# Sine and product of a chunk issued two chunks behind its scaling instead of one

## The chip, the cores and the metric

One NeuronCore of one Trainium2 chip. The metric is the device time of one execution in microseconds; lower is better.

## The reference

A long convolution along the sequence, then a gated feed-forward layer on its output. Shapes: 4 sequences of 12480 positions, 128 channels; the layer has 2048 hidden units; all float32 (the layer's weights arrive as float64).

```python
h_filt = (np.maximum(pos_emb @ w1, 0.0) @ w2) * np.exp(-0.01 * pos)[:, None]
u = x * v
y = irfft(rfft(u, n=2*S) * rfft(h_filt, n=2*S))[:, :S, :]   # causal convolution
x2 = (x * y).reshape(49920, 128)
h = x2 @ w_in            # 128 -> 2048
g = h * np.cos(h)
out = g @ w_out          # 2048 -> 128
```

## The kernel before

The convolution of sequence 0 is done first, alone. From 635 us on, the layer runs over 104 tiles of 480 tokens, each in 16 **chunks** of 128 hidden units, and between its instructions the convolutions of sequences 1 to 3 are issued in small units. Each of those has five stages: U (load x and v, multiply, fold), F1 (first transform), F2 (second transform and product with the filter), I1 and I2 (back). After them comes a stretch with the layer alone, called plain below.

cos(h) is sin(2 pi f), with f the signed distance of h/(2 pi) + 1/4 from its nearest whole number. A chunk therefore goes through all the engines: matmul `ph` on TensorE (PE), scaling `a` on ScalarE (ACT), rounding `k` on VectorE (DVE), fraction `f` on GpSimd (POOL), sine `cs` on ACT, product `gt` on DVE, second matmul into `acc` on PE.

```python
ps_acc = tile_pool(name="ps_acc", bufs=2, space=PSUM)
ps_h = tile_pool(name="ps_h", bufs=4, space=PSUM)      # ph, and the transposes below
ps_c = tile_pool(name="ps_c", bufs=2, space=PSUM)      # the convolution's banks
# ... cut ...
def moe_turn(pool, n):                                 # input of tile n, transposed
    zb = zbs.pop(n)
    pt = ps_h.tile([P, BANK], F32, name="ph")          # borrows a ph
    # ... four transposes into pt, then DVE: at <- pt

def moe_up(pool, n, c):
    ph = ps_h.tile([P, BANK], F32, name="ph")
    nc.tensor.matmul(ph[:, 0:TOK], w_in_sb[:, c * P:(c + 1) * P], ats[n][:, :], ...)
    a = pool.tile([P, TOK], F32, name="a", bufs=3)
    nc.scalar.activation(a[:, :], ph[:, 0:TOK], AF.Identity, bias=quarter[:, 0:1], scale=INV_TWO_PI)
    k = pool.tile([P, TOK], F32, name="k")
    nc.vector.tensor_scalar(out=k[:, :], in0=a[:, :], scalar1=ROUND, scalar2=ROUND,
                            op0=ALU.add, op1=ALU.subtract)
    f = pool.tile([P, TOK], F32, name="f")
    nc.gpsimd.tensor_tensor(f[:, :], a[:, :], k[:, :], op=ALU.subtract)
    return ph, f

def moe_act(pool, ph, f):
    cs = pool.tile([P, TOK], F32, name="cs")
    nc.scalar.activation(cs[:, :], f[:, :], AF.Sin, scale=TWO_PI)
    gt = pool.tile([P, TOK], F32, name="gt", bufs=4)
    nc.vector.tensor_tensor(gt[:, :], ph[:, 0:TOK], cs[:, :], op=ALU.mult)   # last reader of ph
    return gt

# ... cut: moe_store borrows a ph too, for the transposes of a tile's output ...
for i in range(len(steps) + LAG):                      # LAG = 4
    if i < len(steps):
        n, c = steps[i]
        # ... load of tile n + 2 at c == 0 ...
        hidden[i] = moe_up(mpool, n, c)
    if 0 <= i - 1 < len(steps):
        gates[i - 1] = moe_act(mpool, *hidden.pop(i - 1))
    if i >= LAG:
        pn, pc = steps[i - LAG]
        moe_down(pn, pc, gates.pop(i - LAG))
        # ... copy of a finished tile to ot, on ACT ...
    if i < len(steps):
        if c == LAG + 1 and n - 1 in ots:
            moe_store(mpool, n - 1, ots.pop(n - 1))    # at position 5
        if c == NFC // 2 and n + 1 < NALL:
            moe_turn(mpool, n + 1)                     # at position 8
    owed += share
    while owed > 0.0:
        owed -= next(conv, owed)                       # units of the convolution
```

In U, a unit is one multiplication `xt` on DVE, then one sum on POOL and one difference on DVE into `slots`.

## Time and profile before

| | before |
|---|---|
| median time | 4257.37 us (3 runs, 4257.25 to 4261.64) |
| profiled span, granted TensorE clock | 4262.5 us, 0.954 |
| the layer with convolutions between, 635 to 3376 us | 1139 chunks |
| the layer alone, 3376 to 4251 us | 525 chunks, 1.67 us each |

Three ways of reading are used throughout. A row of the busy table by stretch has, after the stretch and its length, the busy time and number of instructions of PE, its weight loads, DVE, ACT and POOL, then the granted clock, the busy share of the DMA engines and their GB/s. A row of the waits says who stood still, what ended it, the total in us, how often, and the longest. A row of the timeline has start, duration, engine, line, operation, what it writes and reads, and in brackets how long its engine had been idle and what ended that. The lines that carry the argument are shown inside the prediction.

### The profile page before, as it was taken

How to read it: one execution, taken by the hardware profiler on the slowest of the kernel's cores; microseconds unless marked ns; L12 is line 12 of the kernel's file. 1: busy time of each engine (PE TensorE's matmuls, PEld its weight loads, DVE VectorE, ACT ScalarE, POOL GpSimd, SP SyncE). 2: the span in 40 equal slices, each digit the busy share in tenths (PEclk: the TensorE clock that was granted, in tenths of full speed). 3: DMA queues.
4: the chain of work that ended last, by engine and by line, in shares of the span. 5: the costliest groups of instructions: out<-in, count | busy, mean ns of one | idle time of the engine just before them, and what ended most of it. 6: DMA issues, size and time to landing. Idle time of an engine off the chain costs nothing.

```text
span 4262.5 us, 49170 instructions
## 1 busy us (share of the span) xinstructions
PE 3916.4 (92%) x13882; PEld 2244.3 (53%) x13882; DVE 3047.8 (72%) x6588; ACT 2415.2 (57%) x4484; POOL 2546.8 (60%) x2311
## 2 busy tenths in 40 slices
PE   5868778999999998998899989988999999999999
PEld 3836673554456653554466634644466644444444
DVE  8657669987778568777776588766675566666666
ACT  1343155775567445655455456644554577777777
POOL 2422347657865457568854476568754577777776
PEclk8557889999999999999999999999999999999999
DMA  3354343112211442012201531022103400000000
GB/s 86 89 167 120 96 136 106 50 52 78 82 51 42 142 142 85 15 50 81 75 12 51 177 112 42 15 73 78 52 15 107 127 19 19 19 19 19 19 19 14
DMA packets 271763, 293.63 MB, mean 69 GB/s; under 512 B 16741, under 2 KB 204101, under 8 KB 271237
## 3 DMA queue, kind: packets, MB, share of 16 engines
q1 hardware_dynamic: 271493, 290.50, 23.6%
q8 instruction: 112, 1.84, 0.2%
q14 instruction: 158, 1.29, 0.1%
HBM read 210.12 MB, written 80.31 MB: 68 GB/s over the span
## 4 chain that ended last, share of the span: by engine, by line
PE 65%; POOL 11%; DVE 10%; ACT 5%; DMA 5%; issue 3%; SPq 0%; DVEq 0%; POOLq 0%; ACTq 0%
PE ph L569 24%; PE acc L591 23%; POOL f L578 6%; POOL slots L369 5%; PE cv L404 4%; PE cv L386 4%; ACT cs L583 3%; PE cv L343 3%; PE ps L343 3%; DVE gt L585 2%; DMA w<-wd 2%; DMA hd<-h 2%; PE ph L116 2%; DVE slots L336 1%; PE ps L386 1%
## 5 line engine op out<-in xcount | busy, mean ns | idle before, releaser
L578 POOL TENSOR_TENSOR f<-a,k 128x480 f32<-128x480 f32 x1664 | 2021.9, 1218 | 1174.9 <-DVE k L575 1174.9
L569 PE MATMUL ph<-at,w_in_sb 128*128 128x480 f32 x3328 | 1647.4, 577 | 102.6 <-DVE gt L585 101.6
L591 PE MATMUL acc<-gt,w_out_sb 128*128 128x480 f32 x3328 | 1618.0, 568 | 0.5 <-DVE gt L585 0.5
L572 ACT ACTIVATE a<-ph,quarter 128x480 f32<-128x480 f32 x1664 | 1094.2, 658 | 750.7 <-PE ph L569 691.8
L585 DVE TENSOR_TENSOR gt<-ph,cs 128x480 f32<-128x480 f32 x1664 | 1091.7, 656 | 476.3 <-ACT cs L583 452.7
L583 ACT ACTIVATE cs<-f 128x480 f32<-128x480 f32 x1664 | 998.4, 600 | 690.6 <-POOL f L578 688.7
L575 DVE TENSOR_SCALAR k<-a 128x480 f32<-128x480 f32 x1664 | 778.8, 468 | 528.3 <-ACT a L572 514.4
L591 PEld LDWEIGHTS acc<-gt,w_out_sb 128*128 128x128 f32 x3328 | 633.8, 190 | 715.5 <-issue 713.5
L569 PEld LDWEIGHTS ph<-at,w_in_sb 128*128 128x128 f32 x3328 | 584.8, 191 | 575.4 <-issue 290.4
L369 POOL TENSOR_TENSOR slots<-slots,t 120x256 f32<-120x256 f32 x384 | 296.6, 795 | 228.2 <-DVE t L368 176.6
L357 PE MATMUL ps<-slots,w 124*120 124x256 f32 x384 | 165.9, 576 | 80.7 <-DVE w L250 45.6
L386 PEld LDWEIGHTS cv<-cs,slots 120*96 120x96 f32 x1536 | 180.5, 168 | 82.0 <-issue 72.1
L357 PE MATMUL cv<-slots,w 124*120 124x256 f32 x576 | 155.3, 390 | 49.7 <-PE acc L591 36.0
L404 PEld LDWEIGHTS cv<-slots,tm 96*104 96x104 f32 x1440 | 173.1, 171 | 46.7 <-issue 36.0
L386 PE MATMUL cv<-cs,slots 120*96 120x120 f32 x1536 | 191.2, 267 | 3.3 <-POOL slots L369 3.3
L404 PE MATMUL cv<-slots,tm 96*104 96x128 f32 x1440 | 178.7, 275 | 11.0 <-DMA tm<-td 7.2
L343 PEld LDWEIGHTS cv<-c,slots 104*124 104x124 f32 x768 | 130.6, 192 | 84.4 <-issue 54.8
L357 PEld LDWEIGHTS ps<-slots,w 124*120 124x120 f32 x384 | 93.0, 268 | 153.0 <-issue 70.5
L357 PEld LDWEIGHTS cv<-slots,w 124*120 124x120 f32 x576 | 98.7, 182 | 134.3 <-PE acc L591 78.0
L343 PE MATMUL cv<-c,slots 104*124 104x192 f32 x768 | 159.5, 330 | 3.2 <-POOL slots L336 2.6
L396 DVE TENSOR_TENSOR slots<-cv,other 96x240 f32<-96x240 f32 x384 | 135.9, 393 | 0.5
L330 POOL TENSOR_TENSOR xt<-xt,vt 104x512 f32<-104x512 f32 x30 | 38.3, 1276 | 137.5 <-DMA vt<-in_v_dram 127.0
(111 smaller groups left out, 2781.8 us busy)
## 6 DMA issues: line engine op xcount, KB each, us to landing
h<-hd SPq DMA_DIRECT2D x192, 240.0 KB
tm<-td SPq DMA_DIRECT2D x90, 312.0 KB
xt<-in_x_dram SPq DMA_DIRECT2D x120, 208.0 KB
vt<-in_v_dram SPq DMA_DIRECT2D x120, 208.0 KB
xs<-in_x_dram SPq DMA_DIRECT2D x120, 208.0 KB
zd<-zs SPq DMA_DIRECT2D x120, 208.0 KB
zb<-zd SPq DMA_DIRECT2D x104, 240.0 KB
out_dram<-ob SPq DMA_DIRECT2D x104, 240.0 KB
```

What stands on the lines that cost most here:

```text
L343: nc.tensor.matmul(ps[0:KE, i * 2 * N1:(i + 1) * 2 * N1], u[:, b, 0:KE, i], c1[0:u.shape[0], :, :].rearrange("p r k -> p (r k)"), start=Tr ...
L357: nc.tensor.matmul(ps[0:N2, i * 2 * D:(i + 1) * 2 * D], w[:, i, :], parts[0:KE, :, k1 + i, :, :], start=True, stop=True)
L369: nc.gpsimd.tensor_tensor(y[:, r], y[:, r], t[:, r], op=op)
L386: nc.tensor.matmul(ps[0:N1, (i * 2 + r) * N2:(i * 2 + r + 1) * N2], parts[0:N2, r, :, b, i], cs[:, r:r + 2, :].rearrange("p c a -> p (c a) ...
L404: nc.tensor.matmul(ps[0:R, i * D:(i + 1) * D], t[:, i, r, :], slots[0:N1, :, place, :], start=(r == 0), stop=(r == 1))
L569: nc.tensor.matmul(ph[:, 0:TOK], w_in_sb[:, c * P:(c + 1) * P], ats[n][:, :], start=True, stop=True)
L572: nc.scalar.activation(a[:, :], ph[:, 0:TOK], AF.Identity, bias=quarter[:, 0:1], scale=INV_TWO_PI)
L575: nc.vector.tensor_scalar(out=k[:, :], in0=a[:, :], scalar1=ROUND, scalar2=ROUND, op0=ALU.add, op1=ALU.subtract)
L578: nc.gpsimd.tensor_tensor(f[:, :], a[:, :], k[:, :], op=ALU.subtract)
L583: nc.scalar.activation(cs[:, :], f[:, :], AF.Sin, scale=TWO_PI)
L585: nc.vector.tensor_tensor(gt[:, :], ph[:, 0:TOK], cs[:, :], op=ALU.mult)
L591: nc.tensor.matmul(accs[n][:, 0:TOK], w_out_sb[:, c, :], gt[:, :], start=(c == 0), stop=(c == NFC - 1))
```

## The change

The sine and the product of chunk i-1 stood behind the scaling of chunk i. The intent is to give POOL one chunk more before ACT needs its f, so that ACT and DVE do not stand at the head of their queues waiting for it. The fraction and its rounding get a third buffer, since they now live longer.

```diff
     LAG = 4
+    SINE_LAG = 2
@@
-        k = pool.tile([P, TOK], F32, name="k")
+        k = pool.tile([P, TOK], F32, name="k", bufs=3)
@@
-        f = pool.tile([P, TOK], F32, name="f")
+        f = pool.tile([P, TOK], F32, name="f", bufs=3)
@@
-            if 0 <= i - 1 < len(steps):
-                gates[i - 1] = moe_act(mpool, *hidden.pop(i - 1))
+            if 0 <= i - SINE_LAG < len(steps):
+                gates[i - SINE_LAG] = moe_act(mpool, *hidden.pop(i - SINE_LAG))
```

All lines of the changed kernel from here on are one further down: line 572 before is 573 after.

## The prediction

> **What bounds the kernel now.** I read the page's busy shares first, then the busy time by stage, then the waits of the stages where TensorE has gaps, then the timeline of one period in each.
>
> ```profile
> PE 3916.4 (92%) x13882; PEld 2244.3 (53%) x13882; DVE 3047.8 (72%) x6588; ACT 2415.2 (57%) x4484; POOL 2546.8 (60%) x2311
> ```
>
> TensorE (PE) leads, but 92% is a mean over stages. The gated layer (1664 chunks of 480 tokens, 16 chunks to a tile, 104 tiles) runs from 635 us to the end. Until about 3376 us the three remaining convolutions are interleaved with it, each in five stages. Busy time of the second convolution's stages, one row each: loading and folding (U), first transform (F1), second transform with product (F2), back transforms (I1, I2), and last the stretch with no convolution left ("plain"). Columns: stretch, length, then busy us of PE, PE's weight loads, DVE, ACT, POOL.
>
> ```profile
> 1543.00:1695.00 152.00, 126.34 (x304) 51.72 (x302) 132.70 (x202) 80.47 (x139) 111.54 (x97) 0.99 0.35 102
> 1696.00:1865.00 169.00, 168.71 (x593) 100.57 (x592) 125.69 (x284) 113.04 (x219) 91.11 (x77) 1.00 0.06 15
> 1869.00:2125.00 256.00, 232.40 (x676) 118.49 (x676) 181.31 (x411) 128.07 (x222) 206.10 (x200) 1.00 0.28 78
> 2135.00:2313.00 178.00, 177.69 (x845) 111.33 (x844) 125.72 (x285) 105.64 (x219) 92.11 (x78) 1.00 0.04 12
> 2320.00:2453.00 133.00, 132.49 (x683) 91.66 (x684) 69.32 (x126) 56.15 (x95) 55.15 (x46) 0.97 0.58 172
> 3400.00:4200.00 800.00, 800.00 (x2165) 387.78 (x2164) 555.27 (x1022) 611.29 (x993) 579.62 (x481) 1.00 0.07 19
> ```
>
> F1, I1, I2 and the plain stretch are full of matmuls; only U (126 of 152) and F2 (232 of 256) have gaps. The activation of line 572 runs once a chunk: 68, 75, 107, 75, 46 and 481 times in these stretches, so a chunk takes 2.24, 2.25, 2.39, 2.37, 2.89 and 1.66 us. The waits of F2 say why it is slow:
>
> ```profile
> ACT cs L583 <- POOL f L578: 112.8, 62, 2.8
> DVE gt L585 <- ACT cs L583: 69.1, 47, 1.7
> ```
>
> and its timeline shows a closed loop:
>
> ```profile
> 2002.07 1.58 POOL L369 TENSOR_TENSOR slots<-slots,t 120x256 f32<-120x256 f32 x2 [0.97 <-PE acc L591]
> ...
> 2003.61 2.55 POOL L578 TENSOR_TENSOR f<-a,k 128x480 f32<-128x480 f32 x2
> ...
> 2005.03 0.60 ACT L583 ACTIVATE cs<-f 128x480 f32<-128x480 f32 x1 [2.75 <-POOL f L578]
> ...
> 2005.66 0.66 DVE L585 TENSOR_TENSOR gt<-ph,cs 128x480 f32<-128x480 f32 x1 [1.72 <-ACT cs L583]
> ...
> 2006.24 0.41 DVE L367 TENSOR_TENSOR slots<-cv,h 120x256 f32<-120x256 f32 x1
> ...
> 2007.13 1.59 POOL L369 TENSOR_TENSOR slots<-slots,t 120x256 f32<-120x256 f32 x2 [0.97 <-PE acc L591]
> ```
>
> POOL's two convolution adds, the fraction f behind them, the sine cs, the product gt, DVE's convolution products behind gt, then POOL's adds again: 5.06 us, for two chunks and one convolution unit.
>
> **What the Trainium skill says.** "PSUM — Partial Sum Buffer", section Engine vs sequencer instructions: the queues of ScalarE, VectorE and GpSimdE are strictly first in, first out, and matmuls keep program order. The trace agrees: ACT stands 2.75 us at a sine that waits for f, with later work behind it. That is what a longer lag removes, and also what makes it dangerous: an older sine now stands behind a newer activation. "Perfetto Trace Analysis", section Identifying Performance Opportunities: a gap that repeats may mean too little PSUM for the next tile. Here the input tile `ph` has four PSUM buffers, which the change does not touch. "SBUF — State Buffer", section Who interferes with whom: a VectorE operation that uses the port pair shared with GpSimd blocks for the whole instruction. The trace agrees: k of line 575 takes 0.41 us in the plain stretch and 1.05 us in U at 1601.73, beside an f at 1601.32. So I take no gain on DVE from the change.
>
> **The change, part by part.** No work is added or removed. In iteration i, ACT had a(i), cs(i-1); it gets a(i), cs(i-2). DVE had k(i), gt(i-1), convolution; it gets k(i), gt(i-2), convolution. The third buffers of k and f only make this legal.
>
> *What it removes.* In F2, cs then needs an f that POOL issued one iteration earlier, so the 5.06 us loop spans three chunks, 1.7 us each, under what PE needs. PE's need: a pair of 480-column matmuls starts every 0.805 us in the plain stretch, so 1.61 us for both layers; an F2 unit has four of 256 columns, 4 x 0.215 = 0.86 us, once in 2.3 chunks by the source's table, 0.37; transposes take 0.85 us a tile, 0.05. Sum 2.04 us. Between the convolutions' first and last matmuls I count 326 chunks in F2 over all three, in 776 us; at 2.04 they would take 665, so at most 111 us is to be had. In U, DVE is the limit: 2.1 us a chunk (union of its busy time) of 2.28; 199 chunks, at most 36 us.
>
> *What it adds.* `ph` of a chunk is held until its gt. The pool hands out the buffer freed first in program order. In the trace before this can be read off: over all chunks, the shortest time from the end of a product to the start of a first-layer matmul is 0.05 us for the product 4 chunks back in most positions of a tile, but 3 back at positions 6, 7, 9 and 10 (from 0), because the transposes at 5 and 8 borrow a `ph`. Following the same rule with lag 2, in iteration i a chunk still needs the product 4 back, but positions 6 and 9 need the one 3 back, and that one is now issued in the iteration just before. So at positions 6 and 9 there is a serial chain from one first-layer matmul to the next: matmul(i-1), a(i-1), cs(i-3), gt(i-3), matmul(i). Its steps stand in the timeline:
>
> ```profile
> 3800.23 0.97 PE L569 MATMUL ph<-at,w_in_sb 128*128 128x480 f32 x2
> ...
> 3801.24 0.66 ACT L572 ACTIVATE a<-ph,quarter 128x480 f32<-128x480 f32 x1
> ...
> 3807.90 0.67 ACT L572 ACTIVATE a<-ph,quarter 128x480 f32<-128x480 f32 x1
> ...
> 3808.56 0.60 ACT L583 ACTIVATE cs<-f 128x480 f32<-128x480 f32 x1
> ...
> 3809.20 0.66 DVE L585 TENSOR_TENSOR gt<-ph,cs 128x480 f32<-128x480 f32 x1
> ```
>
> ```profile
> 1603.18 0.66 DVE L585 TENSOR_TENSOR gt<-ph,cs 128x480 f32<-128x480 f32 x1 [0.40 <-ACT cs L583]
> ...
> 1603.89 1.07 PE L569 MATMUL ph<-at,w_in_sb 128*128 128x480 f32 x2 [0.16 <-DVE gt L585]
> ```
>
> Matmul to a 1.01, a to cs 0.66, cs to gt 0.64, gt to the freed matmul 0.71: **3.02 us**. In the plain stretch these two positions take 2.05 and 2.01 us now (1.61 and the transposes), and PE is full, so nothing is won back. The loss is 0.97 + 1.01, and 0.1 each for a weight load no longer hidden (the pair above takes 1.07, not 0.97): 2.2 us a tile. 525 chunks are 32.8 tiles: **72 us**. The other positions need two iterations for one 3.02 us chain, against 3.22 us of matmuls: this just fits.
>
> In F1 an iteration with a convolution unit and transposes takes PE about 2.7 us, in I1 about 2.8, in I2 about 3.2: stalls of 0.4, 0.3 and 0.1 with the weight load, 28, 28 and 18 of them, some more where an iteration has no unit: **22 us**. In F2 (41 of them) the unit falls in that iteration or not: 0.15 or about 1.2, mean 0.74: 30 us. In U (25) DVE loses perhaps 0.6 each: 15 us.
>
> *Sum.* Plain +72; F1, I1, I2 +22; F2 -111 +30 and 16 for loss in queues not perfectly filled, -65; U -36 +15 and 11 for the port lock, -10. Net **+19 us**, on 4257 is about **4278**. The part before 635 us is not touched.
>
> **The rivals.** First, *the freed loop wins*: the buffers do not bind, and F2 and U give up to 147 us, 3.5%, 4110. For it speaks the 112.8 us wait in F2; against it, that matmuls wait for gt at exactly the predicted positions already with lag 1. If only part of the stalls came, with the full gain, it would be near 4210. Second, *PSUM becomes the bound everywhere*: if the two-iteration chain of 3.02 us stretches beyond 3.22 by DVE's convolution work or the port lock, every chunk pays, and F2 gains nothing: +72 +22 +30 +15 is +139, near 4395. Against it: the convolution stages have 4 us or more of matmuls for two chunks. Third, *nothing moves*, because the engines just shift in time: PE's 92% speaks for it, but the plain stretch would have to stay at 26.6 us a tile.
>
> **Range and chances.** The cost in the plain stretch is the firmest term (within 15 us, if the buffer rule holds), the gains in F2 and U the loosest (35 us either way). I take 4215 to 4345. Two per cent is 85 us: faster needs the first rival outright, 0.03; slower needs most of the second, 0.09; the rest 0.88.
>
> **What would show it.** In the profile after: a plain tile of 28.8 us instead of 26.6, with waits of line 569 for gt of about 1 us at positions 6 and 9 and none elsewhere; PE below 100% there; in F2 the wait of cs for f mostly gone and a chunk at 2.15 to 2.25 us, not 2.39; F1 and I1 some 0.05 us a chunk slower; U near 2.2. I am wrong if the plain tile stays at 26.6 (then buffers are handed out otherwise), if many more positions wait, or if F2 keeps its period because another wait closes the loop.

## The result, and the profile after

The changed kernel took **4286.55 us** (median of 4 runs, 4279.77 to 4293.11), the kernel before 4259.51 us beside it. The ratio is 1.0063, with a 95% interval of 1.0045 to 1.0081. A ratio here is the mean time of one kernel's runs over that of the other's of the same rounds, so it is not quite the ratio of the medians. By the 2% mark that is "the same", as forecast. The forecast was 19 us more than before; it is 27 us more.

The total hides almost everything: one stage became 9% shorter, another stretch 7% longer. First the page's busy shares of the changed kernel, then its busy time by stage, with the second convolution's U, F1, F2, I1, I2 and a piece of the plain stretch, as in the prediction.

```profile
PE 3907.4 (91%) x13882; PEld 2260.8 (53%) x13882; DVE 3141.6 (73%) x6588; ACT 2345.2 (55%) x4484; POOL 2543.2 (59%) x2311
```

```profile
1535.00:1694.00 159.00, 125.77 (x303) 54.95 (x301) 140.86 (x203) 79.28 (x139) 113.95 (x97) 0.96 0.32 98
1695.00:1863.00 168.00, 167.44 (x585) 100.32 (x585) 124.76 (x283) 110.32 (x216) 90.33 (x76) 1.00 0.05 14
1869.00:2104.00 235.00, 224.81 (x675) 120.29 (x673) 205.74 (x412) 128.22 (x223) 203.41 (x200) 1.00 0.30 84
2115.00:2293.00 178.00, 177.31 (x833) 111.03 (x833) 123.39 (x282) 103.69 (x218) 90.17 (x75) 1.00 0.04 12
2301.00:2432.00 131.00, 131.00 (x684) 90.22 (x684) 69.21 (x126) 54.35 (x95) 55.41 (x46) 0.99 0.57 173
3400.00:4200.00 800.00, 759.94 (x2016) 361.29 (x2015) 511.23 (x952) 528.92 (x924) 539.88 (x449) 1.00 0.06 18
```

F2 shrank from 256 to 235 us for the same work. U grew from 152 to 159. In the plain stretch PE fell from 800 busy us of 800 to 760, and did 2016 matmuls instead of 2165 in the same time. PE's share of the whole (92% to 91%) says none of this.

The waits of F2 in the changed kernel:

```profile
ACT a L573 <- PE ph L570: 105.7, 103, 2.7
...
PEld ph L570 <- DVE gt L586: 22.7, 39, 1.2
```

The 112.8 us in which the sine waited for POOL, first in this view before, are gone from it. ACT now waits for matmuls, which is what an engine that is not the limit should do.

The timeline of the plain stretch of the changed kernel, at position 9 of a tile (the chunks of a tile are counted from 0):

```profile
3889.29 0.97 PE L570 MATMUL ph<-at,w_in_sb 128*128 128x480 f32 x2
...
3890.30 0.66 ACT L573 ACTIVATE a<-ph,quarter 128x480 f32<-128x480 f32 x1 [0.46 <-PE ph L570]
3890.86 0.59 ACT L584 ACTIVATE cs<-f 128x480 f32<-128x480 f32 x1
...
3891.48 0.66 DVE L586 TENSOR_TENSOR gt<-ph,cs 128x480 f32<-128x480 f32 x1
...
3892.19 1.07 PE L570 MATMUL ph<-at,w_in_sb 128*128 128x480 f32 x2 [0.72 <-DVE gt L586]
```

This is the serial chain of the prediction: matmul of chunk 8, its a, the sine of chunk 6, the product of chunk 6, and only then the matmul of chunk 9, whose buffer that product freed. Its steps are 1.01, 0.56, 0.62 and 0.71, together 2.90 us, where before 2.01 passed. Averaged over the plain stretch, position 6 takes 2.93 us and position 9 2.88; 7 and 10 take 1.71, since the matmul pair that had waited takes 1.07 us instead of 0.97 (last line above); the other twelve take 1.61 as before. A plain tile takes 28.55 us, against 26.61. Over the whole layer, the matmul starts 0.05 us after the product 3 chunks back in 88 of 102 tiles at position 6 and in 96 at position 9, and at no other position.

For the whole comparison I measured each stage from its first convolution matmul to its last, all three convolutions added (U: from the end of the stage before, and from the layer's first matmul the first time; the few us between the other stages are left out). In us:

| stage (chunks) | before | after | foreseen | found |
|---|---|---|---|---|
| U (199) | 452.8 | 474.1 | -10 | +21 |
| F1 (228) | 506.6 | 512.2 | | +6 |
| F2 (326) | 775.8 | 706.9 | -65 | -69 |
| I1 (228) | 538.3 | 540.9 | | +3 |
| I2 (141) | 397.5 | 399.8 | | +2 |
| F1, I1, I2 together | | | +22 | +11 |
| plain (525) | 874.8 | 938.8 | +72 | +64 |
| sum | 3545.8 | 3572.7 | +19 | +27 |

So the mechanisms of F2 and of the plain stretch came out as forecast, and U has the wrong sign. The experiments test the first two, and look for the third.

### The profile page after: what moved, and what is told of

The parts are those of the page before. It is cut to its first block, busy times and chain, and to the rows that moved or that the text cites. A ratio compares the mean times of both kernels' runs of the same rounds, so it can differ in the third digit from the quotient of the medians.

```text
span 4283.9 us, 50499 instructions
## 1 busy us (share of the span) xinstructions
PE 3907.4 (91%) x13882; PEld 2260.8 (53%) x13882; DVE 3141.6 (73%) x6588; ACT 2345.2 (55%) x4484; POOL 2543.2 (59%) x2311
## 4 chain that ended last, share of the span: by engine, by line
PE 74%; DVE 7%; issue 3%; ACT 2%; DMA 2%; POOL 1%; SPq 0%; DVEq 0%; POOLq 0%; ACTq 0%
PE ph L570 32%; PE acc L592 28%; PE cv L405 4%; PE cv L387 4%; DVE gt L586 4%; PE cv L358 3%; PE cv L344 2%; DVE k L576 2%; PE ps L387 1%; DMA zd<-zs 1%; PE ph L117 1%; ACT a L573 1%; ACT cs L584 1%; DVE slots L337 0%; POOL f L579 0%
## 5 line engine op out<-in xcount | busy, mean ns | idle before, releaser
L570 PE MATMUL ph<-at,w_in_sb 128*128 128x480 f32 x3328 | 1655.3, 579 | 178.7 <-DVE gt L586 175.6
L576 DVE TENSOR_SCALAR k<-a 128x480 f32<-128x480 f32 x1664 | 822.6, 494 | 914.8 <-ACT a L573 891.6
L584 ACT ACTIVATE cs<-f 128x480 f32<-128x480 f32 x1664 | 987.3, 593 | 1.4 <-POOL f L579 0.9
```

## The experiments

**My theory**: the gain in F2 comes from the opened loop over POOL; the loss in the plain stretch comes from four `ph` buffers being one too few at the two positions behind a transpose. **Rivals**: lag 2 costs something everywhere; or the gain in F2 is only work put off; or the buffers alone, not the lag, decide.

| run | edit | us | ratio to before (95%) |
|---|---|---|---|
| e3 | lag 2 only while convolutions run | 4225.09 | 0.9919 (0.9904 to 0.9934) |
| e4 | lag 2 only in F2 | 4191.20 | 0.9839 (0.9824 to 0.9853) |
| e1 | lag 2, transposes in the convolution's banks | 4287.14 | 1.0065 (1.0048 to 1.0082) |
| e2 | lag 1, the same banks | 4399.83 | 1.0331 (1.0316 to 1.0347) |
| e7 | lag 2, five ph | 4158.31 | 0.9758 (0.9744 to 0.9771) |
| e10 | lag 1, five ph | 4297.07 | 1.0083 (1.0068 to 1.0098) |
| e5 | lag 3, four ph (one look) | 6133.0 | single run, state unknown |
| e8 | f only filled, wrong result (one look) | 4161.66 | single run, state unknown |
| e11 | e7, and U's units ahead of the product | 4151.82 | 0.9738 (0.9722 to 0.9755) |
| e9 | e4, lag 1 near the transposes | 4173.84 | 0.9795 (0.9781 to 0.9808) |

Runs were made in three groups, each with its own runs of the kernel before on the same chip (medians 4259.78, 4261.66 and 4261.93). Their stages, in us:

| stage | before | after | e1 | e2 | e4 | e7 | e10 | e11 |
|---|---|---|---|---|---|---|---|---|
| U | 452.8 | 474.1 | 449.6 | 451.5 | 452.6 | 449.4 | 460.1 | 443.6 |
| F1 | 506.6 | 512.2 | 538.3 | 544.6 | 507.0 | 502.4 | 509.3 | 505.3 |
| F2 | 775.8 | 706.9 | 727.1 | 824.8 | 708.4 | 673.6 | 773.5 | 672.6 |
| I1 | 538.3 | 540.9 | 571.1 | 575.2 | 535.5 | 536.4 | 537.0 | 536.4 |
| I2 | 397.5 | 399.8 | 416.4 | 417.7 | 398.1 | 398.3 | 399.5 | 398.3 |
| plain | 874.8 | 938.8 | 874.8 | 874.7 | 874.7 | 886.2 | 897.5 | 886.2 |

### Do the stages add up? (e3, e4)

e3 goes back to lag 1 once the last convolution is done:

```diff
-            if 0 <= i - SINE_LAG < len(steps):
-                gates[i - SINE_LAG] = moe_act(mpool, *hidden.pop(i - SINE_LAG))
+            while acted < len(steps) and acted <= i - lag:
+                gates[acted] = moe_act(mpool, *hidden.pop(acted))
+                acted += 1
@@ convolutions(), after the last one
+            lag = 1
```

> Lag 2 while convolutions run, lag 1 from the end of the last one, ph buffers as before. Theory: the 64 us of the plain stretch come back and nothing else moves: plain tile 26.6, total 4215 to 4230. Rival (the plain stretch pays for something that the convolution leaves behind): tile above 28, total above 4270.

Measured: 4225.09 us; the plain tile is back at 26.61 us, the stretch at 875.7, and the other stages are those of the changed kernel within 2 us. The 64 us of the plain stretch are a cost of lag 2 there and of nothing that came before.

e4 uses the same loop with lag 1, and sets lag to 2 at the start of F2 and back to 1 at its end:

```diff
+        yield "lag", 2
         yield from f2_units(bank, f2_product)
+        yield "lag", 1
```

> Lag 2 in the second-transform stage F2 alone, lag 1 elsewhere. Theory (stages add up, each with its own limit): F2 at 2.17 us a chunk as in the changed kernel, all other stages as before, U back at 2.28: total 4185 to 4200. Rival (the gain of F2 is work put off to the next stage, or U's loss comes from F2's): I1 or U longer by 10 us or more, total above 4210.

Measured: 4191.20 us, F2 708.4 (2.17 us a chunk), U 452.6, everything else as before within 3 us. The gain in F2 is real and is not work put off. The stages can be treated one by one, which is why the forecast could add them.

### Is it the borrowed buffer? (e1, e2)

Both transposes take one of the convolution's two banks instead of a `ph`:

```diff
-        pt = ps_h.tile([P, BANK], F32, name="ph")      # in moe_turn and in moe_store
+        pt = bank()
```

> The changed kernel, with the transposes of a tile's input and output taken from the convolution's two PSUM banks instead of the four ph buffers; lag 2 kept. Theory (the borrowed ph at positions 5 and 8 makes the whole loss of the plain stretch): plain tile 26.6 us instead of 28.55, no wait of a first-layer matmul for gt there, positions 6 and 9 back near 2.05; the plain stretch 64 us shorter, F1, I1 and I2 10 us, F2 20 us shorter; U is open: about 10 us shorter if its loss is those waits, unchanged if it is DVE slowed by POOL. Total 4175 to 4200. Rival (lag 2 itself, the chain of two iterations, slows the plain stretch): plain tile stays at 28.5, total 4275 to 4290. Second rival (the transposes now stall the convolution's banks): plain 26.6 but F1, I1, I2 longer by 10 us or more each.

Measured: 4287.14 us, 100 more than I expected. The plain stretch behaves as the theory says: 26.61 us a tile, 874.8 us, no matmul waits for a product 3 back. U comes down by 24 us. But F1, I1 and I2 became 26, 30 and 17 us longer than in the changed kernel, and F2 20 us longer instead of 20 shorter: the second rival of the expectation is true beside the theory. The timeline of e1 in F1 shows it:

```profile
1712.39 0.60 PE L117 MATMUL cv<-ident,ot 128*120 128x128 f32 x4
1714.31 0.92 PE L344 MATMUL cv<-c,slots 104*124 104x192 f32 x4 [1.31 <-DVE ob L605]
```

The transposes now fill a bank `cv`; the next convolution matmul needs it, and PE stands 1.31 us until DVE has copied it out to `ob`. Two banks are one too few for that user.

> Control: the kernel before (lag 1) with the same move of the transposes to the convolution's banks. Theory: the plain stretch stays at 26.6 us a tile, F2 stays near 2.38 us a chunk since its loop of POOL, sine and product is still closed, total 4235 to 4260. Rival (the move alone is what helps): total below 4210.

Measured for the control at lag 1: 4399.83 us. The move alone is a loss of 140 us; I had expected none, and missed. The plain stretch stays at 874.7 as foreseen; F1, I1 and I2 pay 38, 37 and 20 us; F2 pays 49. So the move is no remedy, and at lag 1 it hurts F2 most. That the loop over POOL has no room there for another wait would explain it, but no run shows it.

### One buffer more (e7, and its control e10)

```diff
-        ps_acc = ctx.enter_context(tc.tile_pool(name="ps_acc", bufs=2, space=PSUM))
-        ps_h = ctx.enter_context(tc.tile_pool(name="ps_h", bufs=4, space=PSUM))
+        ps_acc = ctx.enter_context(tc.tile_pool(name="ps_acc", bufs=1, space=PSUM))
+        ps_h = ctx.enter_context(tc.tile_pool(name="ps_h", bufs=5, space=PSUM))
```

> The changed kernel (lag 2 everywhere) with five ph buffers instead of four and one bank instead of two for the accumulated output, so that all eight banks stay in use and the convolution keeps its two. Theory (a chunk after a transpose waits because four ph buffers are one too few): positions 6 and 9 no longer wait for gt, each back near 2.05 us in the plain stretch; U falls by about 24 us to 450, F1, I1 and I2 by about 10, F2 by 20 to 30. New cost by construction: the first second-layer matmul of a tile waits for the copy of the tile before, an estimated 0.45 us at one position of each tile, 47 us in all. Total 4190 to 4230. Rival (the transposes themselves cause the wait, not the number of buffers): positions 6 and 9 stay at 2.9 us, total above 4300.

Measured: 4158.31 us, ratio 0.9758, faster than both kernels. Positions 6 and 9 of the plain stretch are back at 2.05 and 2.01 us. Position 5 takes 1.96, the foreseen wait for the copy of the finished tile, 0.35 us instead of the estimated 0.45. In F2 a chunk takes 2.06 us, where matmuls need 2.04 by the prediction's sum; U falls by 25 us, F1, I1 and I2 by 16 in all. The count of buffers, not the transposes, made the waits. (The edit also takes one `acc` buffer away; the wait at position 5 is its price, 0.35 us a tile.)

> Control: five ph buffers and one bank for the accumulated output as in the best run so far, but lag 1 as in the kernel before. Theory (in F2 the loop over POOL, sine and product limits at lag 1, not the buffers; in the plain stretch nothing limits but matmuls and the new wait for the copy of a tile): F2 at 2.33 to 2.40 us a chunk, U near 2.26, plain tile 26.9 to 27.3, total 4255 to 4285. Rival (the fifth buffer alone brings the gain and the lag is beside the point): F2 below 2.15, total below 4190.

Measured at lag 1: 4297.07 us. That is 12 us above the range I gave: the wait for the tile's copy is dearer at lag 1 (position 5: 2.30 us in the plain stretch), and U is 460 instead of 450. What the control is for came out: F2 stays at 2.37 us a chunk, and its waits begin as before the change:

```profile
ACT cs L583 <- POOL f L578: 116.6, 63, 2.8
```

So neither edit gives the gain alone. Five buffers at lag 1: 1.0083; lag 2 with four: 1.0063; both: 0.9758. The first of these is no pure count of `ph` buffers: 23 us of it are the plain stretch with its single `acc`.

### The dose (e5)

```diff
-    SINE_LAG = 2
+    SINE_LAG = 3
@@
-        f = pool.tile([P, TOK], F32, name="f", bufs=3)
+        f = pool.tile([P, TOK], F32, name="f", bufs=4)
```

> Dose: lag 3 with the four ph buffers (f four deep). Theory (a first-layer matmul waits for a product issued behind the activation of a chunk before it): with lag 3 every position needs the product issued one iteration before, so the serial chain of 3.0 us binds every chunk: plain tile 46 to 50 us instead of 28.55, total 5600 to 6000. Rival (only the transposes' positions can be hurt, elsewhere matmuls bound): plain tile below 32 us, total below 4450.

Measured in one look: 6133 us, and a plain tile of 52.23 us. The plain positions take 3.06 to 3.18 us each, as the chain says, except 6 and 9, which take 4.50 and 4.41: there the wait for the transposes' own copies stands in series too, which I had left out. Both totals lie somewhat above my ranges. The wait that was worth 175.6 us in the whole changed kernel is now

```profile
PE ph L570 <- DVE gt L586: 1269.0, 1367, 4.2
```

With lag 3, four buffers leave no chunk of distance, and every matmul waits behind the scaling of the chunk before it. A kernel whose PE was 92% busy became 44% longer by a reorder that adds no work.

### Why U became slower (e8, e11)

e1 and e7 show the first part: without the waits behind the transposes U takes 450 us, 25 less than in the changed kernel. But 450 is what it took before the change. In e7, DVE's waits for a sine over the three U fell from 40 us to 1, and yet its busy time rose from 397 to 432 us. The multiplication `xt`, one in each of 90 units, says where it went (after the count: shortest, median and longest duration in ns; first the kernel before, then the changed one):

```profile
L330 DVE TENSOR_TENSOR xt<-xt,vt x90: 693/854/1251, 638.7 to 2600.1; 104x512 f32<-104x512 f32 x90
```

```profile
L331 DVE TENSOR_TENSOR xt<-xt,vt x90: 682/1342/1352, 637.7 to 2586.6; 104x512 f32<-104x512 f32 x90
```

Two rows of the timeline of the kernel before, in U, then two of the changed one:

```profile
1602.86 1.20 POOL L578 TENSOR_TENSOR f<-a,k 128x480 f32<-128x480 f32 x1 [0.35 <-DVE k L575]
...
1603.76 0.85 DVE L330 TENSOR_TENSOR xt<-xt,vt 104x512 f32<-104x512 f32 x1
```

```profile
1606.08 1.21 POOL L579 TENSOR_TENSOR f<-a,k 128x480 f32<-128x480 f32 x1 [0.34 <-DVE k L576]
...
1606.53 1.31 DVE L331 TENSOR_TENSOR xt<-xt,vt 104x512 f32<-104x512 f32 x1
```

Before, f ends at 1604.06 and xt at 1604.61; after, f ends at 1607.29 and xt at 1607.84. Each time xt ends 0.55 us after f. Over all of U this holds for every xt that starts during an f, 78 of 90 before and 87 of 90 after, within 0.006 us. So xt hardly advances until f is done (with nothing beside it, in e8 below, it takes 0.68 us), and close to half of its slice in the changed kernel is standing still. At lag 1 DVE came to xt late, because the product ahead of it had waited for a sine; at lag 2 it comes 0.4 us earlier and stands 0.4 us longer: 0.87 us in the mean before, 1.24 after, in 90 units 33 us of DVE's time; in e7 it is 1.26, 34 us more than before, about as much as DVE's busy time rose there. Its end relative to f is the same at both lags, and standing longer need not cost anything: in the rows of F2 above DVE's busy time rose too, from 181.3 to 205.7 us, and the stage became shorter. So it is shown that the wait for the sine became a wait for f, not that these 33 us are U's loss.

The granted clock explains at most a small part: in the second U it was 0.957 in the changed kernel (159.9 us) and 0.989 before (152.8 us), but e3, also at lag 2 there, had 0.989 and took 157.5 us.

e8 takes away what makes it stand, with a wrong result:

```diff
-        nc.gpsimd.tensor_tensor(f[:, :], a[:, :], k[:, :], op=ALU.subtract)
+        nc.gpsimd.memset(f[:, :], 0.125)
```

> Wrong result on purpose: the changed kernel with POOL's subtraction for f (two SBUF operands read) replaced by a fill of f, which reads nothing. Theory (in U, DVE's multiplication xt and the scaling k stand still while POOL's f runs): xt falls from 1.24 us to below 0.8, k in U from 0.62 to below 0.5, and U from 2.38 us a chunk to 2.0 to 2.15; positions 6 and 9 of the plain stretch keep their 2.9 us. Rival (U is slow only because of the ph waits): U stays above 2.3 us a chunk although xt is shorter.

Measured in one look: the row of xt in e8 has, after the count, the shortest, median and longest duration in ns.

```profile
L331 DVE TENSOR_TENSOR xt<-xt,vt x90: 674/678/693, 638.4 to 2469.7; 104x512 f32<-104x512 f32 x90
```

xt takes 0.68 us every time, k in U 0.46, and U 1.85 us a chunk, better than I expected (2.0 to 2.15), though positions 6 and 9 keep their 2.91 and 2.87 us in the plain stretch. This is no pure test: the fill is also shorter on POOL than the subtraction (0.50 us in the median, not 1.21), it does not wait for k, and it runs during xt in one unit of 90 alone. So e8 shows xt with nothing beside it, not beside a harmless operation, and how much of the gain in U is the standing still stays open. POOL was busy for 114 of 159 us of the U shown above. (Where the texts of e8 and e11 say "scaling k", the rounding k is meant.)

e11 leaves all work in place and only lets xt start first. It is e7 with the convolution's unit issued ahead of the sine and product while in U:

```diff
                 hidden[i] = moe_up(mpool, n, c)
+            if early:                       # set by the generator in stage U
+                owed += share
+                while owed > 0.0:
+                    owed -= next(conv, owed)
+                owed -= share
             if 0 <= i - SINE_LAG < len(steps):
```

> Lag 2 with five ph buffers, and in U the convolution's step is issued ahead of the sine and product of the iteration, so that DVE's xt multiplication follows the scaling k at once and starts before POOL's f. Theory (whichever of xt and f starts first makes the other stand still, and DVE is the fuller engine in U): xt falls from 1.26 to 0.55 to 0.75 us, U from 2.26 to 1.9 to 2.1 us a chunk, total 4100 to 4135; f waits instead. Rival (the product now comes late and its ph with it, or the lock moves to the next operation): U at 2.2 or more, total 4150 or more.

Measured: 4151.82 us, U 443.6 (2.23 us a chunk), only 6 us better than e7. xt did fall to 0.68, but the rows of `xt` and of the difference behind it in e11 show where it went:

```profile
L331 DVE TENSOR_TENSOR xt<-xt,vt x90: 676/678/708, 640.2 to 2518.5; 104x512 f32<-104x512 f32 x90
...
L337 DVE TENSOR_TENSOR slots<-xt x90: 411/1424/1434, 643.3 to 2523.3; 104x256 f32<-104x256 f32 x90
```

The difference took 0.95 us in the median before and takes 1.42 now, since f starts right behind xt; f itself now takes 1.58 us in such places. The theory was right on who makes whom stand, the rival on what it is worth: the wait moved on by one operation. What is left of U's gap is open; moving f or the sums to another engine would be the next thing to try, and was not.

### A cheaper schedule (e9)

e4 with lag 1 again at positions 4 to 8, in F2:

```diff
+            near = 1 if i < len(steps) and LAG <= c <= NFC // 2 else lag
-            while acted < len(steps) and acted <= i - lag:
+            while acted < len(steps) and acted <= i - near:
```

> Lag 2 in F2 alone as in the earlier run, and there lag 1 again at positions 4 to 8 of each tile, so that the product 3 back has been issued two iterations before where transposes borrow a ph. Theory: the waits at positions 6 and 9 in F2 shrink, F2 from 2.17 to 2.10 to 2.14 us a chunk, total 4165 to 4185. Rival (at lag 1 the loop over POOL closes again for a third of the chunks and takes as much as it gives): F2 2.17 or more, total 4190 to 4215.

Measured: 4173.84 us, F2 697.5 us, 2.13 a chunk. In F2, position 6 takes 2.72 us instead of the 3.25 of e4, but position 9 still 3.11 instead of 3.20: of the two waits that were to shrink without a fifth buffer, one did. e7 gains more in F2 (673.6 us).

## Why the prediction was right, and where not

- **F2 is bound by a closed loop over POOL**: right. Foreseen -65 us, found -69; the wait for f left the view. The parts came out too: without the waits behind the transposes (e7) F2 is 102 us shorter (foreseen 95), and those waits cost 33 (foreseen 30). e10 shows that it is the lag and not buffers that opens the loop.
- **Positions 6 and 9 need the product 3 back, through a serial chain of 3.02 us**: right. The chain measured 2.90; the sine starts 0.56 us after a, not 0.66. Foreseen 72 us in the plain stretch, found 64. e3, e7 and e5 remove, remove and widen it.
- **The rule by which buffers are handed out, read off the trace of lag 1**: right; the waits after the change sit at exactly the two positions derived from it, and had I taken a plain rotation of four instead, six positions would have waited.
- **F1, I1 and I2**: the right sign, half the size (+11, not +22).
- **U**: the step that failed, "U -36 +15 and 11 for the port lock, -10". The waits behind the transposes were 25, not 15, as e1 and e7 show by removing them. With them removed U is 3 us shorter than before, so next to nothing of the gain came: DVE's wait for the sine went (40 us), but DVE's busy time rose by 35, and xt alone stands 0.38 us longer for f in each of 90 units, 34 us. The room was misread as well: the union of DVE's busy time was 2.00 us a chunk (397 us for 199 chunks), not 2.1, so 56 us and not 36 seemed to be had. I had looked at k for the lock, which changed little (0.67 to 0.62 us in U), and not at the instruction whose start the change moved into the middle of f. What sets U's length now is open: e11 took the standing away from xt, and the difference behind it stood instead.
- **The total**: 4257 + 19 is 4276, where the prediction wrote 4278. That it was only 8 us short of the rise is partly luck: U was missed by 31, and the other three rows by 23 the other way.
- **The rivals**: none came true as a whole. "PSUM becomes the bound everywhere" is what lag 3 does, and "the freed loop wins" is what the fifth buffer does.

## What to carry to other kernels

When you delay a stage of a software pipeline, count the buffers between its ends, and count them at the tightest place, not on the average; a buffer borrowed twice a tile decided here whether the same reorder cost 0.6% or gained 2.4%. Read how buffers are handed out from the trace, by looking for the distance at which a start follows an end by a constant 0.05 us. And when a change makes one engine start earlier, ask what other engines run at that moment: here POOL's f made DVE's xt stand.

## What the Trainium skill lacked or had wrong

- "SBUF — State Buffer", section Who interferes with whom, is borne out: the later starter stands for the whole instruction (165 of 180 xt start during an f, and each of these ends 0.55 us after it). Whether a fill, which reads nothing, leaves xt alone was not tested, since in e8 the two overlap once in 90 units; k, with one SBUF input, does stand for the fill (0.61 us in the median in the 127 cases that start during one, 0.41 otherwise). The page does not say that reordering moves the wait to the next operation: 0.95 to 1.42 us for the difference in e11.
- "Perfetto Trace Analysis", section Identifying the Most-Contended Engine, calls occupancy a fair measure for Vector of how close it is to roofline. Here it is not: DVE's busy time in the stretch of F2 shown rose from 181.3 to 205.7 us and in that of U from 132.7 to 140.9 us for the same work, since the slice of a blocked instruction includes its standing still.
- No page that I read says how a software-pipeline lag uses up PSUM buffers, or that a short-lived borrower shortens the distance for two later users. The numbers here: 26.61, 28.55 and 52.23 us a tile at lag 1, 2 and 3 with four buffers, and 26.96 at lag 2 with five.
